# Local attention steps in pairs on four quarters of TensorE, in a fused attention and two-layer feed-forward kernel

## Chip, cores and metric

The program runs on 1 core of one Trainium2 chip. The metric is device time in microseconds of that core, from the start of the program to its end; lower is better. Three runs of the kernel before have a median of 943.49 µs (941.63 to 943.52).

## The reference

```python
def _attn_ref(q, k, v):                      # B, H, S, D = 4, 8, 576, 64
    factor = 4
    scale = 1.0 / np.sqrt(D)
    q_d, k_d, v_d = (mean over 4 neighbouring tokens of q, k, v)
    out_up = np.repeat(sm_attn(q_d, k_d, v_d), factor, axis=2)
    mask = np.abs(pos[:, None] - pos[None, :]) < factor
    scores = np.where(mask, scale * q @ k.T, -1e9)
    out_local = softmax(scores) @ v
    return out_up + out_local
...
x = attn_out.transpose(0, 2, 1, 3).reshape(2304, 512)
g = x @ w_gate
x = (g * sigmoid(g) * (x @ w_val)) @ w_out   # 512 -> 1536 -> 512
h = np.maximum(x @ w_in, 0.0)
out = (h * h) @ w_out2                       # 512 -> 2048 -> 512
```

Per head there is a "global" attention over 144 pooled tokens, and a "local" one in which a query sees only the keys fewer than 4 positions away. Their sum, 2304 tokens of 512, goes through two feed-forward layers. All of it is float32.

## The kernel before

**Precision.** Feed-forward products are made of three single-pass products each (`three`, lines 1045 to 1047): high part by high part, high by low, low by high. Those lines carry most of TensorE's time. The attention matmuls take float32 operands directly; in the trace one such matmul is two records.

**Local attention.** The 576 tokens of a batch are cut into ten blocks of 56 or 58 queries (`EDGES`, `BLOCKS`), each with a window of 64 keys. A block has 8 heads: four pairs `hp`, and in a pair one head on partitions 0–63 and one on 64–127 (`h2`). One step (`local_task`, line 613) does one or two blocks: `nb` is 1 or 2. Per batch there are six steps, of blocks (0,1), (2,3), (4) in the first half and (5), (6,7), (8,9) in the second. The stages of a step, in order:

- `scores` (line 635): for batches 0 and 1 (`MASK_PE` is 2) the mask first enters the bank by a bf16 matmul (L644); then, per block and head pair, two matmuls of 64 rows by 64 columns (L649), the first on rows 0–63 into output partitions 0–63, the second on rows 64–127 into output partitions 64–127. For batches 2 and 3 VectorE adds the mask instead (`masked`, L661).
- the softmax stages on VectorE and ScalarE (lines 550 to 588),
- `trans` (L686): two 128x128 transposes per block on TensorE, and `turned` (L694): eviction to SBUF by ScalarE,
- `pv` (line 696): per block eight matmuls of 64 rows by 64 columns over 58 or 56 queries (L707), again alternating between rows and output partitions 0–63 and 64–127,
- `to_x` (L725): VectorE adds the pooled attention `g` and writes the tile `xt`.

The values come by `values`: one DMA for batch 0 (L674), two per block for the other batches (L681), into one of two `vw` buffers. The load may start once the step's scores have been issued. Transposes wait for `turn`: the global steps of the same half must have come far enough.

The global steps (`global_tasks`, `global_task`) have scores in L797, which alternate between rows 0–63 and 64–127 and write output partitions 0–71 of one bank for the first and of another for the second, and value products in L835, which use rows 0–71 and alternate between output partitions 0–63 and 64–127 of one bank.

**What sets the order.** Nothing is scheduled at run time. A planner inside the program (`Order`, `Task`, `Stage`) simulates the engines with costs written in the code, and emits the instructions in the order that its simulation gives; each engine then executes its own list in order. Every stage has an engine, a cost and the buffers that it takes and gives: four PSUM banks `att`, two `gv`, two `y`; five `p` tiles, two `pt`, two `vw`, two `xt`. Attention has priority on TensorE up to 2 µs at a stretch (`ATT_MAX`), then products go first. A local step's scores are planned at 0.63 µs per block and 0.737 with masks, its value products at 0.64 per block. A DMA is planned at its size over 70e3 elements per µs, plus a flight of 1.7 µs (`FLIGHT`) and 3.5 µs of slack (`SLACK`); the values of two blocks count as 1.87 µs. Between 40 and 100 µs the planner fills long waits for a bank with dummy matmuls (`bank`, L81). The first 40 µs have other dummies (L1251).

**Weights.** Weights arrive as words that ScalarE and VectorE turn into high and low tiles (`bit_stages`, L367 to L384; `pair_task`, L1355 to L1366). While attention runs, some of this work is done ahead, and the tiles are written to DRAM and fetched later: `N_FIRST` groups of eight tiles of the second layer (two calls of `pair_task` each, on two sources each), and `N_PUT` blocks of five tiles of the second half of the first layer (one `pair_task` and one `w_task`; spilled to `f_sp`). The other blocks are converted after attention has ended (`late_`), and the other groups later still.

**Order of the stages over the span.** Batch 0's first half and its global steps stand in the first 45 µs with little else; from then to 270 µs attention is interleaved with the first half of the first layer; then come the second half of the first layer and the second layer, which have no attention.

Of the kernel before, what the change touches and what calls it, by code (L numbers as in the profile page):

```python
# [1 line left out]

# [1 line left out]

# [15 lines left out]
B, H, S, D = 4, 8, 576, 64  # L20
NTOK, DM, FF1, FF2 = B * S, H * D, 1536, 2048
HP = H // 2
# [3 lines left out]
WIN = 64  # L26
# [33 lines left out]
HALF0 = (0, S - HALF)  # L60
# [3 lines left out]
def attn_moe_kernel(ctx: ExitStack, tc: tile.TileContext, qT, kT, vw, vin, vp, qp, kp, qs, ks, vs, maskc, masks, identc, wB, wC, out):  # L64
    nc = tc.nc
# [32 lines left out]
    def dma(size):  # L98
        return size / RATE
# [27 lines left out]
    def after(ts):  # L127

        return max([0.0] + [t.ready for t in ts]) if all(t.done for t in ts) else None
# [392 lines left out]
    def x_of(token):  # L522
        return max(t for t in range(NT1) if X_AT[t] <= token)
# [87 lines left out]

    early_room = []

    def local_task(b, i, ins, due, bls=(0, 1), early=False):

        u = {}
        first, last = early and i == 0, early and i == 2
# [2 lines left out]
        def room(k, size=None):  # L620
# [5 lines left out]
        nb, b0 = len(bls), bls[0]  # L626
# [5 lines left out]
        if len(set(kinds)) == 1:  # L632
            runs = [(0, n, kinds[0])]

        def scores():
            half = int(t00 >= S // 2)
            q, k, o = q_t[b, half], k_t[b, half], HALF0[half]
# [7 lines left out]
            for c, (_, _, q0, w0) in enumerate(blocks):  # L645
                for hp in range(HP):
                    for h2 in range(2):
                        r = slice(64 * h2, 64 * h2 + 64)
                        nc.tensor.matmul(  # L649
                            u["s"][r, c * HP + hp],  # L650
                            q[r, hp, q0 - o : q0 - o + WIN],
                            k[r, hp, w0 - o : w0 - o + WIN],
                            start=not mask_pe,
                            stop=not mask_pe or c * HP + hp == n - 1,
                        )

        def masked():
            u["p"] = p_tile(128, n, WIN)
# [11 lines left out]
        def values():  # L670
            v = room(10, 8 * D) if last else att.tile([128, 8 * D], F32, tag="vw", bufs=N_V, name="vw")
            if b < NB:
                u["v"] = v.rearrange("p (a h l d) -> p l a h d", a=2, h=2, d=D)
                nc.sync.dma_start(out=v, in_=vw[b * NPAIR + i].rearrange("p a h l d -> p (a h l d)"))  # L674
                return
            u["v"] = v.rearrange("p (l h a d) -> p l a h d", h=2, a=2, d=D)
            heads = vs[b - NB].rearrange("p f -> (p f)").rearrange("(r h t d) -> r t h d", r=2, h=4, d=D)
            for r in range(2):
                for bl, (_, _, _, w0) in zip(bls, blocks):
                    o = v[64 * r : 64 * r + 64].rearrange("p (l h d) -> p l h d", l=2, d=D)[:, bl]  # L680
# [15 lines left out]
        def pv():  # L696
            for t in tiles:
                x_tile(t)
            ps = u["ps"] = bank("att")
            pt = u["pt"].rearrange("p (b a h k) -> p b a h k", b=nb, a=2, h=2)  # L700
            for c, (t0, t1, q0, _) in enumerate(blocks):
                for hpp in range(2):
                    for h2 in range(2):
                        for r in range(2):
                            rr = slice(64 * r, 64 * r + 64)
                            o = (2 * h2 + hpp) * 128 + t0 - t00
                            nc.tensor.matmul(  # L707
                                ps[rr, o : o + t1 - t0],
                                u["v"][rr, bls[c], hpp, h2, :],
                                pt[rr, c, hpp, h2, t0 - q0 : t1 - q0],  # L710
                                start=True,
                                stop=True,
                            )

        def to_x():
            at = t00
# [14 lines left out]
                at = end  # L731

        tiles = range(x_of(b * S + t00), x_of(b * S + t11 - 1) + 1)

        def g_need():
            return [t for c in range(t00 * 2 // S, (t11 - 1) * 2 // S + 1) for t in g_tasks[b, c]]

        def ready():
            when, room = after([v_in] + g_need()), x_room(tiles)
            return None if when is None or room is None else max(when, room)  # L740

        def turn():

            return 0.0 if early or all(t.at > len(t.stages) - 4 for t in g_need()) else None

        v_take = () if last else ("v",)
        v_in = Task([Stage("d", dma(128 * 512) * (1 if b < NB else 2), values, v_take, cond=lambda: task.ready)], due)
        if mask_pe:
            cost, share = 0.737 * nb, 0.74
            softmax = softmax_stages(u, n, 128, WIN, "s", float(D) ** -0.5, 1, False, ("att",))  # L750
        else:
            cost, share = 0.63 * nb, 0.68
            softmax = [Stage("v", dve(n * WIN), masked, (), ("att",))]
            softmax += softmax_stages(u, n, 128, WIN, "p", 1.0, 1, False, ())
        p_take, pt_take, pt_give = ("p",), ("pt",), ("pt",)
        if early:
            p_take, pt_take = ("xs",) * 3 * first, ()
            pt_give = tuple(lambda k=k: ("xs", early_room[k][0]) for k in range(3)) if last else ()
        task = Task(
            [Stage("t", cost, scores, ("att",) + p_take, (), lambda: after(ins + [consts]), share)]  # L760
            + softmax
            + [
                Stage("t", 0.22 * nb, trans, ("att",) + pt_take, p_take[-1:] * (not early), turn, 0.98),
                Stage("a", act(n * WIN, True), turned, (), ("att",)),
                Stage(
                    "t", 0.64 * nb, pv, ("att",), pt_give + v_take, ready, 0.62
                ),
                Stage("v", dve(232 * nb), to_x, (), ("att",)),
            ],
            due,  # L770
            then=[v_in],
        )
        for t in tiles:
            x_parts[t].append(task)
        return task

    def global_tasks(b, ins, due, combos, end=False):

# [89 lines left out]
            g_tasks[b, qc].append(task)  # L868
        return task

    att_tasks = {}

    def x_due(token):
        tile = token / T1
# [41 lines left out]
    def queue_att(b):  # L916
# [69 lines left out]
            ]  # L986
            return list(glob_tasks[b, qc])

        halves = ((0, (0, 1)), (1, (0, 1)), (2, (0,))), ((2, (1,)), (3, (0, 1)), (4, (0, 1)))
        ts = globals_(0) + globals_(1) if b >= NB else []  # L990
        for qc in range(2):
            first = globals_(qc) if b < NB else []
            early = EARLY if first and qc == 0 else 0.0
            loc_tasks[b, qc] = [local_task(b, i, ins[qc], due[qc] - early, bls, early > 0) for i, bls in halves[qc]]
            ts += loc_tasks[b, qc] + first if early else first + loc_tasks[b, qc]
        queues["att"] += ts
        att_tasks[b] = ts


    xh_t, x_at, x_tasks, y_t, downs = {}, {}, {}, {}, []  # L1000
# [320 lines left out]
    last_scores = lambda: 0.0 if all(t.at for t in att_tasks[B - 1]) else None  # L1321
# [855 lines left out]
    def rows(t, r0, c):  # L2177
        return t[r0 + 2 * c : r0 + 2 * c + 2].rearrange("r p d -> p r d")
# [265 lines left out]
```

## Time and profile before

| | |
|---|---|
| median of 3 runs | 943.49 µs (941.63 to 943.52) |
| the profiled execution's own time | 944.18 µs |
| its span in the profile | 942.4 µs |
| granted TensorE clock, mean | 0.999 of full speed |
| instructions | 22566 |

How to read it: the span runs from the first to the last instruction of the program in the profile; the execution's own time has 1.8 µs more. Busy time is the time in which an engine has an instruction in flight, and matmuls are pipelined, so records overlap and 100% busy doesn't mean that no more would fit. PE is TensorE's matmuls, PEld its weight loads, DVE VectorE, ACT ScalarE, POOL GpSimd, SP the queue that issues most DMAs. L649 is line 649 of the kernel. In rows by window the five busy times stand in the order PE, PEld, DVE, ACT, POOL.

### The profile page before, as it was taken

What the parts mean: (1) busy time and instruction counts of PE and PEld (TensorE: products, weight loads), DVE (VectorE), ACT (ScalarE), POOL (GpSimd) and SP (SyncE); (2) the same over time, 40 slices, a digit from 0 to 9 for tenths busy, and PEclk for the clock granted to TensorE, in tenths of its full rate; (3) what the DMA queues carried; (4) which work ended last, traced back from release to release, by engine and by line L of the source; (5) the groups of instructions that cost most, each with busy time, mean ns of one, the idle gap of its engine ahead of it and who ended that gap; (6) DMA issues with size and microseconds to landing.
All of it is one profiled execution on the core that took longest, in us unless ns stands there. A gap on an engine that the chain in (4) does not pass through costs nothing.

```text
span 942.4 us, 22566 instructions
## 1 busy us (share of the span) xinstructions
PE 931.2 (99%) x8929; PEld 907.0 (96%) x8929; DVE 757.3 (80%) x1875; ACT 584.5 (62%) x1368; POOL 23.8 (3%) x31
## 2 busy tenths in 40 slices
PE   8999999999999999999999999999999999999997
PEld 6888999999999999999999999999999999999997
DVE  6998969878978878788796999978777666776865
ACT  3878667657667888456542675757565645555553
POOL 0102102000000000000000000000000000000000
PEclk9999999999999999999999999999999999999999
DMA  9998969586678857166553638624315864516131
GB/s 278 262 286 225 243 186 239 179 270 183 225 269 312 265 172 252 50 220 204 187 185 101 211 138 312 244 81 180 126 77 178 316 230 171 180 67 247 47 133 68
DMA packets 101205, 183.82 MB, mean 195 GB/s; under 512 B 22380, under 2 KB 60012, under 8 KB 101100
## 3 DMA queue, kind: packets, MB, share of 16 engines
q1 hardware_dynamic: 97644, 174.42, 54.8%
q0 software_dynamic: 3456, 7.96, 4.8%
q8 instruction: 70, 1.15, 0.5%
q14 instruction: 35, 0.29, 0.1%
HBM read 120.75 MB, written 61.60 MB: 193 GB/s over the span
## 4 chain that ended last, share of the span: by engine, by line
PE 92%; DVE 2%; ACT 2%; DMA 2%; SPq 1%; issue 0%; DVEq 0%
PE gv L1045 11%; PE gv L1047 10%; PE gv L1046 10%; PE y L1045 8%; PE y L1046 8%; PE y L1047 8%; PE att L1983 6%; PE att L1982 6%; PE att L1981 6%; PE att L1046 3%; PE att L1047 3%; PE att L1045 3%; PE att L707 2%; PE att L797 2%; PE att L649 1%; PE y L1251 1%
## 5 line engine op out<-in xcount | busy, mean ns | idle before, releaser
L1045 PE MATMUL gv<-xs,wg 128*128 128x256 f32 x880 | 250.4, 285 | 0.1
L1046 PE MATMUL gv<-xs,wg 128*128 128x256 f32 x880 | 246.9, 281 | 0.0
L1047 PE MATMUL gv<-xs,wg 128*128 128x256 f32 x880 | 246.9, 281 | 0.0
L1045 PEld LDWEIGHTS gv<-xs,wg 128*128 128x128 f32 x880 | 166.2, 189 | 2.1 <-issue 0.4
L1046 PEld LDWEIGHTS gv<-xs,wg 128*128 128x128 f32 x880 | 166.1, 189 | 0.0
L1047 PEld LDWEIGHTS gv<-xs,wg 128*128 128x128 f32 x880 | 166.0, 189 | 0.0
L2132 ACT ACTIVATE f<-rr 128x256 fp32r<-128x256 f32 (+2 forms) x200 | 88.1, 467 | 62.9 <-PE att L1983 25.7
L1983 PE MATMUL att<-wg,f 128*128 128x256 f32 x432 | 122.5, 284 | 0.5 <-DVE f L2135 0.4
L1982 PE MATMUL att<-wg,f 128*128 128x256 f32 x432 | 122.0, 282 | 0.0
L1981 PE MATMUL att<-wg,f 128*128 128x256 f32 x432 | 121.7, 282 | 0.3 <-ACT f L2132 0.3
L2135 DVE TENSOR_TENSOR f<-rr,f 128x512 fp32r<-128x512 f32 (+2 forms) x200 | 94.0, 488 | 27.2 <-ACT f L2132 26.5
L2056 ACT ACTIVATE rr<-rr 128x512 f32<-128x512 f32 (+1 forms) x144 | 80.2, 557 | 31.4 <-DVE rr L2059 29.2
L1045 PE MATMUL y<-xs,wg 128*128 128x256 f32 x336 | 94.6, 281 | 1.1 <-ACT ys L1228 1.1
L1046 PE MATMUL y<-xs,wg 128*128 128x256 f32 x336 | 94.5, 281 | 0.0
L1047 PE MATMUL y<-xs,wg 128*128 128x256 f32 x336 | 94.4, 281 | 0.0
L1981 PEld LDWEIGHTS att<-wg,f 128*128 128x128 f32 x432 | 81.8, 189 | 0.7 <-ACT f L2132 0.7
L1983 PEld LDWEIGHTS att<-wg,f 128*128 128x128 f32 x432 | 81.2, 188 | 1.4 <-DVE f L2135 1.3
L1982 PEld LDWEIGHTS att<-wg,f 128*128 128x128 f32 x432 | 81.5, 189 | 0.0
L2141 DVE TENSOR_TENSOR rr<-rr 128x256 f32<-128x256 f32 (+1 forms) x160 | 62.3, 393 | 7.0 <-ACT rr L2056 4.7
L1045 PEld LDWEIGHTS y<-xs,wg 128*128 128x128 f32 x336 | 63.6, 189 | 1.4 <-ACT ys L1228 1.3
L1047 PEld LDWEIGHTS y<-xs,wg 128*128 128x128 f32 x336 | 63.5, 189 | 0.0
L1046 PEld LDWEIGHTS y<-xs,wg 128*128 128x128 f32 x336 | 63.5, 189 | 0.1
(149 smaller groups left out, 2317.2 us busy)
## 6 DMA issues: line engine op xcount, KB each, us to landing
wst<-wB SPq DMA_DIRECT2D x36, 512.0 KB, 4.9
w_sp<-tmp SPq DMA_DIRECT2D x36, 512.0 KB, 3.8
wg<-w_sp SPq DMA_DIRECT2D x36, 512.0 KB, 5.1
wst<-wC SPq DMA_DIRECT2D x32, 512.0 KB, 5.0
y_sp<-ys SPq DMA_DIRECT2D x29, 512.0 KB, 4.5
xf_sp<-xs SPq DMA_DIRECT2D x24, 512.0 KB, 2.7
xs<-xf_sp SPq DMA_DIRECT2D x24, 512.0 KB, 5.4
ys<-y_sp SPq DMA_DIRECT2D x20, 512.0 KB, 6.7
```

The lines of the kernel that those rows point to most:

```text
L707: nc.tensor.matmul(ps[rr, o : o + t1 - t0], u["v"][rr, bls[c], hpp, h2, :], pt[rr, c, hpp, h2, t0 - q0 : t1 - q0], start=True, stop=True,)
L797: nc.tensor.matmul(us[h2]["s"][:, ci], q, kd_t[b][r, hp, :], start=start, stop=stop)
L1045: nc.tensor.matmul(o, w[:, 0], x[:, 0], start=start, stop=False, skip_group_check=more)
L1046: nc.tensor.matmul(o, w[:, 0], x[:, 1], start=False, stop=False, skip_group_check=more)
L1047: nc.tensor.matmul(o, w[:, 1], x[:, 0], start=False, stop=stop, skip_group_check=more)
L1981: nc.tensor.matmul(o, h, w[:, 0], start=first and not again and c == 0, stop=False, skip_group_check=again)
L1982: nc.tensor.matmul(o, h, w[:, 1], start=False, stop=False, skip_group_check=again)
L1983: nc.tensor.matmul(o, l, w[:, 0], start=False, stop=end, skip_group_check=again)
L2056: return lambda: nc.scalar.activation(out=whole(f, c0), in_=whole(f, c0), func=func)
L2132: nc.scalar.activation(out=fac(k, 0), in_=source(), func=AF.Copy)
L2135: nc.vector.tensor_tensor(out=fac(k, 1), in0=source(), in1=fac(k, 0).bitcast(F32), op=ALU.subtract)
L2141: go = lambda: nc.vector.tensor_tensor(out=o(), in0=a(), in1=b(), op=op)
```

## The change

Two local steps become two lanes of one pair. In batches 1 to 3 the pairs are blocks (0,1) with (2,3), (4) with (5), and (6,7) with (8,9); in batch 0 only the last two steps are paired, and the other steps go through the same code with one lane. A pair has one scores stage: the matmuls of the lanes alternate, and lane 1 writes its output into the other half of the partitions (`h2 ^ lane`) and into a bank of its own, so that rows 0–63 feed output partitions 0–63 for lane 0 and 64–127 for lane 1, and rows 64–127 the other way round. Head pairs of lane 1 are swapped as well (`hp ^ lane`), and its values are loaded with the halves of the partitions exchanged, so that after the value products, exchanged once more, each head stands where it stood. Softmax, transposes and `to_x` stay one per lane. The value products of both lanes are one stage again, which takes two banks and waits for both lanes' values, for all global steps that either lane needs and for room in the `xt` tiles. Transposes of a pair also wait until the value products of the pair before have been issued (`val_before`). In batch 0 lane 1's values are two DMAs instead of one. The planner's costs are 0.63 per block of a lane for the scores of one or two lanes, plus 0.107 per block and lane with masks, and 0.64 for the values.

The constants of the weights change from `N_FIRST, N_DIRECT, N_PUT = 4, 2, 1` to `3, 2, 2`.

```diff
-N_FIRST, N_DIRECT, N_PUT = 4, 2, 1
+N_FIRST, N_DIRECT, N_PUT = 3, 2, 2
...
+        def score(at):
...
+            for h2 in range(2):
+                nc.tensor.matmul(
+                    u["s"][rows(h2 ^ lane), c * HP + (hp ^ lane)],
+                    q[rows(h2), hp, q0 - o : q0 - o + WIN],
+                    k[rows(h2), hp, w0 - o : w0 - o + WIN],
...
+                if lane:
+                    for r in range(2):
+                        nc.sync.dma_start(out=v[rows(r)], in_=whole[rows(1 - r)])
+                else:
+                    nc.sync.dma_start(out=v, in_=whole)
...
-                    nc.sync.dma_start(out=o, in_=heads[r, w0 : w0 + WIN])
+                    nc.sync.dma_start(out=o, in_=heads[r ^ lane, w0 : w0 + WIN])
...
+        def value(at):
...
+            for r in range(2):
+                o = (2 * h2 + hpp) * 128 + t0 - t00
+                nc.tensor.matmul(
+                    u["ps"][rows(r ^ lane), o : o + t1 - t0],
+                    u["v"][rows(r), bls[c], hpp, h2, :],
+                    pt[rows(r), c, hpp, h2 ^ lane, t0 - q0 : t1 - q0],
...
+    def local_task(b, parts, ins, due, early=False):
+        lanes = [local_lane(b, i, bls, lane, early) for lane, (i, bls) in enumerate(parts)]
...
+        def scores():
+            for x in lanes:
+                x.masks()
+            for at in range(n):
+                for x in lanes:
+                    x.score(at)
+
+        def pv():
+            for x in lanes:
+                x.begin()
+            for at in range(4 * nb):
+                for x in lanes:
+                    x.value(at)
+
+        def ready():
+            when, room = after(v_in + mids + g_need), x_room(tiles)
+            return None if when is None or room is None else max(when, room)
+
+        def turn():
+
+            if before and not early and not before.done:
+                return None
+            return 0.0 if early or all(t.at > len(t.stages) - 4 for t in g_need) else None
+
+        cost = 0.63 * nb + nl * 0.107 * nb * (b < MASK_PE)
...
+        v_in = [Task([Stage("d", x.load, x.values, v_take, cond=lambda: head.ready)], due) for x in lanes]
+        head = Task([Stage("t", cost, scores, ("att",) * nl + p_take, (), lambda: after(ins + [consts]), 0.7)], due)
...
+        val = Task([Stage("t", 0.64 * nb, pv, ("att",) * nl, pt_give + v_take * nl, ready, 0.7)], due)
+        ends = [Task([Stage("v", dve(232 * nb), to_x, (), ("att",), lambda: after([val]))], due) for x in lanes]
...
-        halves = ((0, (0, 1)), (1, (0, 1)), (2, (0,))), ((2, (1,)), (3, (0, 1)), (4, (0, 1)))
+        both = (0, 1)
+        ends_ = [(3, both), (4, both)]
+        if b < NB:
+            lanes = [[(0, both)], [(1, both)], [(2, (0,))]], [[(2, (1,))], ends_]
+        else:
+            lanes = [[(0, both), (1, both)]], [[(2, (0,)), (2, (1,))], ends_]
```

## Rows read from the trace of the kernel before

**Rows 1.** The page, part 1: busy µs, share of the span, instructions.

```profile
PE 931.2 (99%) x8929; PEld 907.0 (96%) x8929; DVE 757.3 (80%) x1875; ACT 584.5 (62%) x1368; POOL 23.8 (3%) x31
```

**Rows 2.** Windows, all engines: stretch, length, busy (instructions); then clock, DMA share, GB/s.

```profile
40.00:75.00 35.00, 34.98 (x455) 31.28 (x456) 33.12 (x94) 27.31 (x82) 3.43 (x4) 1.00 0.95 299
75.00:270.00 195.00, 194.50 (x2438) 182.39 (x2437) 163.96 (x430) 130.31 (x345) 15.63 (x18) 1.00 0.76 217
270.00:345.00 75.00, 75.00 (x642) 75.00 (x641) 62.26 (x135) 62.66 (x126) 0.00 (x0) 1.00 0.80 274
```

**Rows 3.** Waits of PE: waiter <- releaser, µs, times, longest.

```profile
PE att L707 <- DMA vw<-vs: 0.2, 1, 0.2
```

**Rows 4.** Lines, PE: busy µs, mean ns, then idle before.

```profile
L649 PE MATMUL att<-kT,qT 64*64 64x64 f32 x640 | 23.2, 221 | 1.3 <-DMA qT<-qT 1.3
...
L707 PE MATMUL att<-pt,vw 64*64 64x58 f32 (+1 forms) x560 | 20.4, 221 | 0.2 <-DMA vw<-vs 0.2
...
L81 PEld LDWEIGHTS <-zeros 128*128 128x128 bf16 x28 | 2.6, 97 | 0.5 <-issue 0.2
```

**Rows 5.** Timeline, PE, 96.2–97.9, 104.0–106.4, 267.8–269.4 µs: start, length, line, tiles, records.

```profile
96.39 0.28 PE L1047 MATMUL y<-hh,wg 128*128 128x256 f32 x1
96.60 1.14 PE L707 MATMUL att<-pt,vw 64*64 64x58 f32 x32
...
105.80 0.39 PE L1045 MATMUL gv<-xs,wg 128*128 128x256 f32 x1
106.02 0.28 PE L1046 MATMUL gv<-xs,wg 128*128 128x256 f32 x1
106.14 0.28 PE L1047 MATMUL gv<-xs,wg 128*128 128x256 f32 x1
...
267.99 1.14 PE L707 MATMUL att<-pt,vw 64*64 64x58 f32 x32
```

**Rows 6.** Chain that ended last, in order of time: start, length, what.

```profile
46.68 0.61 PE att L649 x16
...
47.61 1.08 PE att L649 x32
...
143.41 2.01 PE att L649 x64
```

**Rows 7.** Timeline, PE, from 50.970 to 51.079; then to 51.090 and 51.137 alike.

```profile
50.97 0.27 PE L649 MATMUL att<-kT,qT 64*64 64x64 f32 x2
...
50.97 0.33 PE L649 MATMUL att<-kT,qT 64*64 64x64 f32 x4
```

**Rows 8.** Timeline, PE, 73.740 to 73.859 and 73.870; 125.180 to 125.366 and 125.380 µs.

```profile
73.75 0.28 PE L835 MATMUL att<-pt,vd 72*64 72x72 f32 x2
...
73.75 0.35 PE L835 MATMUL att<-pt,vd 72*64 72x72 f32 x4
...
125.19 0.35 PE L797 MATMUL att<-kd,qd 64*72 64x144 f32 x2
...
125.19 0.47 PE L797 MATMUL att<-kd,qd 64*72 64x144 f32 x4
```

**Rows 9.** Lines by form, DVE, weight conversion: busy µs, mean ns.

```profile
L379 DVE SCALAR_TENSOR_TENSOR wf<-wst,bits 128x512 int32<-128x512 int32 x68 | 46.5, 685 | 3.2 <-ACT wst L376 2.7
...
L1366 DVE TENSOR_TENSOR wf<-wf 128x256 f32<-128x256 f32 x88 | 36.8, 418 | 0.8
...
L1359 DVE TENSOR_TENSOR tmp<-wf,tmp 128x512 fp32r<-128x512 f32 x39 | 26.7, 684 | 4.6 <-ACT tmp L1355 4.1
```

**Rows 10.** DMA issues: queue, count, KB each, median µs to landing.

```profile
f_sp<-tmp SPq DMA_DIRECT2D x4, 512.0 KB, 5.0
```

**Rows 11.** Line L681: issues, ns min/median/max; and µs to landing.

```profile
L681 SPq DMA_DIRECT2D vw<-vs x60: 596/616/1705, 79.7 to 261.6; - x60
...
DMA to landing us min/median/max: 2.3/3.0/7.2
```

**Rows 12.** Waits of SP's queue: waiter <- releaser, µs, times, longest.

```profile
SPq L681 <- PE att L707: 14.2, 5, 6.9
```

More of the change, by code (lines that the diff above doesn't have):

```diff
@@ L1 @@
 from contextlib import ExitStack
+from types import SimpleNamespace
 import numpy as np
@@ L625, in room, with rows @@
             return flat[:, k : k + (size or n * WIN)]
-        nb, b0 = len(bls), bls[0]
+        def rows(r):
+            return slice(64 * r, 64 * r + 64)
+        nb = len(bls)
         n = nb * HP
@@ L633, in local_task, with masks @@
             runs = [(0, n, kinds[0])]
-        def scores():
-            half = int(t00 >= S // 2)
-            q, k, o = q_t[b, half], k_t[b, half], HALF0[half]
+        def masks():
             u["ps"] = bank("att")
@@ L644, in scores @@
                 nc.tensor.matmul(u["s"][:, c0:c1], ident_b, m, start=c0 == 0, stop=False)
[L645 to L655, printed above, removed]
+        def score(at):
+            half = int(t00 >= S // 2)
+            q, k, o = q_t[b, half], k_t[b, half], HALF0[half]
+            c, hp = at // HP, at % HP
+            _, _, q0, w0 = blocks[c]
+            for h2 in range(2):
[3 more added lines that the diff above has]
+                    k[rows(h2), hp, w0 - o : w0 - o + WIN],
+                    start=not mask_pe,
+                    stop=not mask_pe or at == n - 1,
+                )
         def masked():
@@ L673, in values @@
                 u["v"] = v.rearrange("p (a h l d) -> p l a h d", a=2, h=2, d=D)
-                nc.sync.dma_start(out=v, in_=vw[b * NPAIR + i].rearrange("p a h l d -> p (a h l d)"))
+                whole = vw[b * NPAIR + i].rearrange("p a h l d -> p (a h l d)")
+                if lane:
[3 more added lines that the diff above has]
+                    nc.sync.dma_start(out=v, in_=whole)
                 return
@@ L733, in local_task @@
         tiles = range(x_of(b * S + t00), x_of(b * S + t11 - 1) + 1)
-        def g_need():
-            return [t for c in range(t00 * 2 // S, (t11 - 1) * 2 // S + 1) for t in g_tasks[b, c]]
+        g_need = [t for c in range(t00 * 2 // S, (t11 - 1) * 2 // S + 1) for t in g_tasks[b, c]]
+        if mask_pe:
+            softmax = softmax_stages(u, n, 128, WIN, "s", float(D) ** -0.5, 1, False, ("att",))
+        else:
+            softmax = [Stage("v", dve(n * WIN), masked, (), ("att",))]
+            softmax += softmax_stages(u, n, 128, WIN, "p", 1.0, 1, False, ())
@@ new lines, in local_lane @@
+        load = dma(128 * 512) * (1 if b < NB else len(bls))
+        return SimpleNamespace(**locals())
+    def local_task(b, parts, ins, due, early=False):
+        lanes = [local_lane(b, i, bls, lane, early) for lane, (i, bls) in enumerate(parts)]
+        nb, n, nl = lanes[0].nb, lanes[0].n, len(lanes)
+        tiles = range(lanes[0].tiles[0], lanes[-1].tiles[-1] + 1)
+        g_need = list(dict.fromkeys(t for x in lanes for t in x.g_need))
+        before = val_before[0]
+        def scores():
[10 more added lines that the diff above has]
+                    x.value(at)
@@ L748, in local_task @@
[L748 to L755, printed above, removed]
-        if early:
-            p_take, pt_take = ("xs",) * 3 * first, ()
-            pt_give = tuple(lambda k=k: ("xs", early_room[k][0]) for k in range(3)) if last else ()
@@ L759, in local_task @@
[L759 to L772, printed above, removed]
@@ L773, in local_task @@
-        for t in tiles:
-            x_parts[t].append(task)
-        return task
+            if before and not early and not before.done:
+                return None
+            return 0.0 if early or all(t.at > len(t.stages) - 4 for t in g_need) else None
+        cost = 0.63 * nb + nl * 0.107 * nb * (b < MASK_PE)
+        p_take, pt_take, pt_give, v_take = ("p",) * nl, ("pt",), ("pt",) * nl, ("v",)
+        if early:
+            p_take, pt_take = ("xs",) * 3 * lanes[0].first, ()
+            pt_give = ()
+            if lanes[0].last:
+                pt_give = tuple(lambda k=k: ("xs", early_room[k][0]) for k in range(3))
+                v_take = ()
@@ new lines, in local_task @@
+        v_in = [Task([Stage("d", x.load, x.values, v_take, cond=lambda: head.ready)], due) for x in lanes]
+        head = Task([Stage("t", cost, scores, ("att",) * nl + p_take, (), lambda: after(ins + [consts]), 0.7)], due)
+        mids = []
+        for x in lanes:
+            x.softmax[0].cond = lambda: after([head])
+            mids.append(
+                Task(
+                    x.softmax
+                    + [
+                        Stage("t", 0.22 * nb, x.trans, ("att",) + pt_take, () if early else ("p",), turn, 0.98),
+                        Stage("a", act(n * WIN, True), x.turned, (), ("att",)),
+                    ],
+                    due,
+                )
+            )
@@ L777, in global_tasks @@
+        val = Task([Stage("t", 0.64 * nb, pv, ("att",) * nl, pt_give + v_take * nl, ready, 0.7)], due)
+        ends = [Task([Stage("v", dve(232 * nb), x.to_x, (), ("att",), lambda: after([val]))], due) for x in lanes]
+        head.then = [*v_in, *mids, val, *ends]
+        if not early:
+            val_before[0] = val
+        for x, end in zip(lanes, ends):
+            for t in x.tiles:
+                x_parts[t].append(end)
+            att_ends[b].append(end)
+        return head
     def global_tasks(b, ins, due, combos, end=False):
@@ L869, in global_task @@
         return task
-    att_tasks = {}
+    att_tasks, att_heads, att_ends = {}, {}, {b: [] for b in range(B)}
     def x_due(token):
@@ L993, in queue_att @@
             early = EARLY if first and qc == 0 else 0.0
-            loc_tasks[b, qc] = [local_task(b, i, ins[qc], due[qc] - early, bls, early > 0) for i, bls in halves[qc]]
+            loc_tasks[b, qc] = [local_task(b, x, ins[qc], due[qc] - early, early > 0) for x in lanes[qc]]
             ts += loc_tasks[b, qc] + first if early else first + loc_tasks[b, qc]
+        if b >= NB:
+            loc_tasks[b, 0].append(loc_tasks[b, 1][0])
         queues["att"] += ts
-        att_tasks[b] = ts
+        att_heads[b] = ts
+        att_tasks[b] = ts + att_ends[b]
     xh_t, x_at, x_tasks, y_t, downs = {}, {}, {}, {}, []
@@ L1320, in attn_moe_kernel @@
     turned_all = lambda: after(sum(att_tasks.values(), sum(x_parts, [])))
-    last_scores = lambda: 0.0 if all(t.at for t in att_tasks[B - 1]) else None
+    last_scores = lambda: 0.0 if all(t.at for t in att_heads[B - 1]) else None
     late_ = Task([apart("tmp", 5, last_scores), apart("bits", 1), Stage(None, 0.0, late, (), (), turned_all)])
```

32 lines of the change are left out of this document (11 added, 21 removed).

## The prediction

> **What bounds the kernel now.** I read the engines' shares first: TensorE 99% of the span, VectorE 80%, ScalarE 62% [rows 1]. Then busy time by stretch, since a share over the whole span hides stages. In 75–270 µs, where batches 1 to 3 pass through attention beside the first feed-forward layer, TensorE is busy 194.50 of 195 µs at full granted clock; VectorE stands at 163.96, the 16 DMA engines at 0.76. In 40–75 µs VectorE is at 33.12 of 35 and DMA at 0.95: there three resources are nearly full together. In 270–345 µs TensorE still has 75.00 of 75 [rows 2]. Third, the waits of TensorE: the value products (L707) waited for their `vw` loads 0.2 µs, once, in the whole run [rows 3]. So from 75 µs on TensorE's own instructions set the pace, and what is taken from them should leave the end of the program, while the 75 µs of 270–345, products alone and without a gap, show that it isn't short of work [rows 2].
>
> How much stands in the two lines that change: the score matmuls (L649) make 640 records and 23.2 µs of busy time, the value products (L707) 20.4 µs for batches 0 (second half) to 3 [rows 4]. The first three steps of batch 0 stay single in the change.
>
> **What a burst costs.** These matmuls come in bursts. A burst of 32 records starts 0.21 µs after the last product where products follow each other at 0.12, and the second product behind a burst comes 0.22 after the first instead of 0.12 [rows 5]. Inside, 16 records take 0.61, 32 take 1.08, 64 take 2.01 µs [rows 6]: (2.01 − 0.61)/48 = 29.2 ns per record and 0.14 fixed. With 0.09 before and 0.10 behind, a separate burst has 0.33 µs of fixed cost.
>
> Why 29.2 ns? Two records start within 11 ns of each other (two in flight at 51.079 µs, four at 51.090), and then no other until after 51.137; the modelled end moves by 0.06 µs [rows 7]. So a round is about 58 ns with one record on each of the two quarters in use; each quarter needs 58 ns per record, and issuing takes 7 to 11 of it. The sequencer has room for two more records in each round.
>
> Would two more quarters run beside them? Two halves of that are in the trace. L835 puts both records on the same rows and on different column halves: two in flight, then four within 11 ns, 0.07 later. L797 puts them on different rows and on the same output partitions of two banks: again pairs [rows 8]. The change needs both at once, which no row shows. Bounds for a round of four: 58 ns (free) and 117 (they take turns, as now). I take 58, the end nearest to both rows.
>
> The Trainium skill, page "TensorE: Matmul & The Clock Gate", Part 3, section "The mechanism", says that a weight load overlaps matmuls in flight only when the row group differs; with quarters in the order 0/0, 1/1, 0/1, 1/0 of rows and columns that would make the second pair queue behind the first and save the fixed costs alone. The column-half pairs of L835 in [rows 8] disagree with it. The same page, Part 1, section "Wait — 56ns, not 53.3ns?", gives a floor of about 25 ns from start to start; by it a round of four would be 100 ns and the sum over the records 272 × 17 = 4.6 instead of 15.9 µs. The pairs within 11 ns in [rows 7] disagree with that as well.
>
> **The sum.** Pairs: one in batch 0 (16 rounds), three in each of batches 1 to 3 (16 + 8 + 16). So 136 rounds of two vanish for scores and 136 for values, and as many rounds of four stay: 272 × 58.4 ns = 15.9 µs. Bursts: I count 16 score and 17 value bursts between 47.5 and 269 µs, the first at 47.61 in [rows 6], the last at 267.99 in [rows 5]; ten of each remain, 13 × 0.33 = 4.3, less where two stand beside each other already; I take 4. Mask matmuls, transposes, softmax, the eviction by ScalarE and the additions into `xt` keep their count and size: 0. Together 20 µs off TensorE.
>
> What doesn't reach the end: batch 0's pair falls into 47–70 µs, where the planner put 28 dummy matmuls (L81) because nothing was ready [rows 4]; its share, 16 of 136 rounds twice plus its bursts, 2.5 µs, only makes more of those. Net 17.5.
>
> The redivided weights (one group of eight tiles fewer in `N_FIRST`, one block of five tiles more in `N_PUT`) move conversion work. A group costs VectorE 4 × 0.685 + 8 × 0.418 + 6 × 0.684 + 2 × 0.418 = 11.0 µs, a block 2 × 0.685 + 4 × 0.418 + 3 × 0.684 + 0.418 for its pair and 0.685 + 0.684 for the third weight, 6.9 [rows 9]. So VectorE has 4.1 µs less before attention ends. In 75–270 its load goes from 164/195 to 160/178 = 90%, which stays under TensorE. In exchange 2.25 MB more goes out and comes back, five issues each way at 5.0 µs to landing [rows 10], in a stretch with DMA at 0.80 [rows 2]: hidden by the products of 270–345, and without that cover late by the 5.0 µs of one landing. I take 0.
>
> Added waits: a value burst now needs both lanes' `vw` buffers, which are all there are, so the next pair's loads (eight issues of 0.6 µs on the sync queue, 3.0 median and 7.2 at most to land [rows 11]) can start only behind it. Batch 0's pair has one issue more than now, 0.6 at that row's price, on a queue that TensorE doesn't wait for there. The next pair's transposes also wait for it (`turn`). Behind a waiting value burst stand the products of TensorE, behind a waiting load the weight and q/k loads of the queue, which is held 14.2 µs in 5 such waits already [rows 12]. Bounds: 0 if the products that the planner puts between cover it, 3 µs per pair if not (4.9 + 7.2 against the 9 µs that the planner's own load cost gives two lanes), 27 in all. The 0.2 µs of [rows 3] is the nearest row: 0.5.
>
> Sum: 944.18 (the profiled execution: span 942.4 and 1.8 around it) − 17.5 + 0.5 = 927.2; the median of the runs is 0.7 lower, so **926.5 µs**.
>
> **Rivals.** *Partial rate or partial cover:* a round of four takes 87 to 100 ns, or VectorE's 90% turns into TensorE waits in 75–120 µs. With 87 the record sum is 272 × 30 = 8.2, 7.7 less: 934; with 100 it is 11.3 less: 938. For: VectorE is at 33.12 of 35 just before. Against: TensorE was busy 99.7% of 75–270 beside it [rows 2], and nothing in [rows 7] shows such a step. The 25-ns floor of the Trainium skill's page above would give the 938. *Quarters take turns:* 117 ns per round; only 4 µs of fixed cost goes, 1.5 of it under dummies and waits: 941. This is the case in which the change doesn't do what it says; against it stand the pairs of [rows 8], for it that no row has all four. The rule on row groups of the Trainium skill's page above would give this case. *Slower, by the value loads:* TensorE stands at each of nine paired value bursts for `vw`, 3 µs each: 926.5 + 27 = 953. It decides from 17/9 = 1.9 µs per pair upwards. For: two buffers, both taken; [rows 12]. Against: [rows 3], and the 75 µs of products in hand at 270 µs [rows 2].
>
> **Numbers.** Full rate with small waits 0.60 (922–931); partial 0.20 (931–939); turns 0.10 (939–943); slower 0.10 (943–955). The range 919 to 940 leaves out the last two and reaches 7 below the forecast for fixed costs of 4.3 fully won, batch 0's share won too, and 4 µs of better cover. 0.2% of this kernel, 1.9 µs, is about what a measurement can tell from no change; turns falls half inside it. Faster 0.84, same 0.06, slower 0.10.
>
> **What would show it.** Right: the score and value lines have fewer, denser bursts; 64 records of a pair in about 1.08 µs (14.6 ns each), four starts within some 25 ns and then a gap to 58; TensorE still full from 75 to 330 µs; the last value burst near 250 µs instead of 267.99. Wrong: 64 records in 2.0 µs (turns), 1.5 (partial); waits of the value matmuls on `vw` over 5 µs in sum; L81 dummies well over 28; VectorE at its limit with TensorE idle between 75 and 200 µs; or idle TensorE around 330–360 µs on late weights.

## The result, and the profile after

The changed kernel takes 931.43 µs (median of 4 runs, 931.01 to 931.92) against 943.5 before: a ratio of 0.9876, 95% interval 0.9859 to 0.9893, 12.1 µs faster. The forecast was 926.5 within 919 to 940. Direction and range held. Up to the end of attention the sum held too; behind it the kernel loses some 3 µs again, in stages for which the sum had taken 0.

In the changed kernel the scores are L657, the value products L720, the mask matmuls L649, the dummies L82, the products L1099 to L1101 and, in the second layer, L2035 to L2037. The page, part 1, answers to [rows 1]:

```profile
PE 914.3 (98%) x8950; PEld 892.1 (96%) x8950; DVE 756.1 (81%) x1875; ACT 584.6 (63%) x1368; POOL 23.7 (3%) x31
```

The same windows as in [rows 2], and two later ones:

```profile
40.00:75.00 35.00, 34.34 (x463) 30.57 (x462) 32.78 (x92) 28.00 (x82) 2.17 (x3) 1.00 0.96 287
75.00:270.00 195.00, 193.25 (x2569) 183.34 (x2569) 167.23 (x439) 132.35 (x350) 15.58 (x18) 1.00 0.77 218
270.00:345.00 75.00, 73.87 (x627) 73.46 (x627) 60.81 (x131) 60.83 (x122) 0.00 (x0) 1.00 0.76 256
345.00:400.00 55.00, 53.56 (x451) 53.16 (x450) 46.04 (x109) 32.52 (x71) 0.00 (x0) 1.00 0.56 202
500.00:600.00 100.00, 98.23 (x822) 97.32 (x821) 92.72 (x217) 66.09 (x142) 0.00 (x0) 1.00 0.69 237
```

The later two in the kernel before:

```profile
345.00:400.00 55.00, 53.87 (x455) 53.46 (x454) 44.62 (x107) 36.70 (x77) 0.00 (x0) 1.00 0.45 149
500.00:600.00 100.00, 99.58 (x837) 98.83 (x836) 86.87 (x208) 57.53 (x125) 0.00 (x0) 1.00 0.54 191
```

TensorE is still nearly full everywhere. New gaps are 1.75 µs in 75–270, 1.3 at 363 µs and 1.4 more in 500–600; the 1.1 in 270–345 is a wait that the kernel before has in 345–400. Lines of PE, as in [rows 4]:

```profile
L657 PE MATMUL att<-kT,qT 64*64 64x64 f32 x640 | 14.1, 222 | 0.9 <-DMA qT<-qT 0.9
...
L720 PE MATMUL att<-pt,vw 64*64 64x58 f32 (+1 forms) x560 | 11.0, 221 | 1.8 <-issue 1.8
...
L82 PE MATMUL gv<-zeros 128*128 128x256 bf16 x39 | 4.6, 273 | 0.0
...
L82 PE MATMUL att<-zeros 128*128 128x256 bf16 x10 | 1.3, 274 | 0.0
```

As many records as before, 640 and 560, stand in 14.1 µs instead of 23.2 and in 11.0 instead of 20.4; 49 dummies instead of 28. The chain of work (start, length, what), as in [rows 6]:

```profile
84.73 1.09 PE att L657 x64
89.89 0.62 PE att L657 x32
...
96.69 1.09 PE att L657 x64
97.78 0.92 PE att L720 x63
98.71 1.75 issue
...
254.73 1.09 PE att L720 x64
```

64 records now take the 1.09 µs that 32 took, and 32 take 0.62 where 16 took 0.61 [rows 6]: rounds of four at the length of rounds of two. The last value burst starts at 254.73 µs; the forecast had it near 250. The timeline from 130.70 to 130.80 µs shows one round, four starts together (compare [rows 7]):

```profile
130.75 0.28 PE L720 MATMUL att<-pt,vw 64*64 64x58 f32 x4
```

The chain shows something else: one value burst that follows a score burst directly stops for 1.75 µs before its last record, for nothing that the profile names. The waits of PE, and those of the sync queue for `vw` (compare [rows 3] and [rows 12]):

```profile
PE att L720 <- issue: 1.8, 1, 1.8
PE att L1099 <- ACT h L1859: 1.3, 1, 1.3
PE att L2035 <- ACT wg L1409: 1.2, 1, 1.2
```

```profile
SPq L694 <- PE att L720: 30.0, 5, 18.5
```

In this row the queue stands twice as long as before; in the kernel before, 8.2 µs more of that line's waits are put down to the transposes (L686), which the changed kernel doesn't have. No matmul of TensorE waited for `vw`.

### The profile page after: what moved, and what is told of

The parts are those of the page before. It is cut to its first block, busy times and chain, and to the rows that moved or that the text cites. A ratio compares the mean times of both kernels' runs of the same rounds, so it can differ in the third digit from the quotient of the medians.

```text
span 929.2 us, 22649 instructions
## 1 busy us (share of the span) xinstructions
PE 914.3 (98%) x8950; PEld 892.1 (96%) x8950; DVE 756.1 (81%) x1875; ACT 584.6 (63%) x1368; POOL 23.7 (3%) x31
## 4 chain that ended last, share of the span: by engine, by line
PE 94%; DVE 3%; ACT 1%; issue 1%; DMA 1%; SPq 0%; DVEq 0%
PE gv L1099 11%; PE gv L1101 11%; PE gv L1100 11%; PE y L1099 9%; PE y L1100 8%; PE y L1101 8%; PE att L2037 6%; PE att L2036 6%; PE att L2035 6%; PE att L1100 3%; PE att L1101 3%; PE att L1099 3%; PE att L843 2%; PE att L657 1%; PE att L720 1%; PE att L881 1%
## 5 line engine op out<-in xcount | busy, mean ns | idle before, releaser
L1099 PE MATMUL gv<-xs,wg 128*128 128x256 f32 x880 | 250.6, 285 | 0.0
L1101 PE MATMUL gv<-xs,wg 128*128 128x256 f32 x880 | 247.2, 281 | 0.1
L1099 PEld LDWEIGHTS gv<-xs,wg 128*128 128x128 f32 x880 | 166.4, 189 | 1.9 <-issue 0.6
L1101 PEld LDWEIGHTS gv<-xs,wg 128*128 128x128 f32 x880 | 166.2, 189 | 0.3 <-DVE wg L427 0.3
L2186 ACT ACTIVATE f<-rr 128x512 fp32r<-128x512 f32 (+2 forms) x200 | 88.2, 467 | 62.1 <-PE att L2037 24.2
L2035 PE MATMUL att<-wg,f 128*128 128x256 f32 x432 | 121.8, 282 | 1.5 <-ACT wg L1409 1.2
L2037 PE MATMUL att<-wg,f 128*128 128x256 f32 x432 | 122.6, 284 | 0.1
L1099 PE MATMUL y<-xs,wg 128*128 128x256 f32 x336 | 94.5, 281 | 1.1 <-ACT ys L1282 1.1
L1101 PE MATMUL y<-xs,wg 128*128 128x256 f32 x336 | 94.5, 281 | 0.0
L2035 PEld LDWEIGHTS att<-wg,f 128*128 128x128 f32 x432 | 81.9, 190 | 1.9 <-ACT wg L1409 1.4
L2037 PEld LDWEIGHTS att<-wg,f 128*128 128x128 f32 x432 | 81.2, 188 | 1.0 <-DVE f L2189 0.8
L1099 PEld LDWEIGHTS y<-xs,wg 128*128 128x128 f32 x336 | 63.6, 189 | 1.3 <-ACT ys L1282 1.3
L1101 PEld LDWEIGHTS y<-xs,wg 128*128 128x128 f32 x336 | 63.6, 189 | 0.0
```

The costliest lines, as they stand in the source:

```text
L1099: nc.tensor.matmul(o, w[:, 0], x[:, 0], start=start, stop=False, skip_group_check=more)
L1101: nc.tensor.matmul(o, w[:, 1], x[:, 0], start=False, stop=stop, skip_group_check=more)
L2035: nc.tensor.matmul(o, h, w[:, 0], start=first and not again and c == 0, stop=False, skip_group_check=again)
L2037: nc.tensor.matmul(o, l, w[:, 0], start=False, stop=end, skip_group_check=again)
L2186: nc.scalar.activation(out=fac(k, 0), in_=source(), func=AF.Copy)
```

## The experiments

Each kernel below is the changed kernel with the edit shown, or the kernel before where that is said; all ratios are to the kernel before on the same chip.

### Two quarters for both lanes

```diff
-        lanes = [local_lane(b, i, bls, lane, early) for lane, (i, bls) in enumerate(parts)]
+        lanes = [local_lane(b, i, bls, 0, early) for lane, (i, bls) in enumerate(parts)]
```

> The changed kernel with one edit: both lanes of a pair use lane 0's two quarters, and nothing is exchanged; the planner's costs, the order of the work and the division of the weights stay as changed. If the gain is the second pair of quarters: the 64 records of a pair take about 2.0 us instead of 1.09, the 272 rounds of 58 ns come back on TensorE, and all but batch 0's share (which then takes the place of dummies) shows: 14 us more, 945 us, with a range of 942 to 948, not faster than the kernel before. If the gain came from pairing alone (fewer separate bursts, another order): 931 to 934.

946.14 µs, ratio 1.0024 (1.0015 to 1.0034): 14.7 slower than the changed kernel. Its chain:

```profile
86.62 2.01 PE att L657 x64
...
99.96 2.01 PE att L657 x64
101.97 1.86 PE att L720 x64
```

So with this division of the weights nothing is left of the gain without the second pair of quarters: pairing by itself ends 2.6 µs slower than before, though it has fewer bursts. The rival that put the gain on pairing is out. One limit: the planner still counts 1.26 µs for these 64 records, which here take 2.01, so the order is one made for four quarters; a plan made for two wasn't tested.

### Lane after lane

```diff
-            for at in range(n):
-                for x in lanes:
+            for x in lanes:
+                for at in range(n):
                     x.score(at)
...
-            for at in range(4 * nb):
-                for x in lanes:
+            for x in lanes:
+                for at in range(4 * nb):
                     x.value(at)
```

> The changed kernel with one edit: in the two loops over a pair's matmuls all of lane 0 is issued before lane 1, so that the two lanes still use four quarters but don't alternate in the program. If TensorE takes its matmuls nearly in order, with room for a few waiting ones: 64 records take 2.0 us, and the time goes to 945 (942 to 948). If it could look 32 records ahead, 64 records would stay at 1.1 and the time at 931 to 932.

941.47 µs, ratio 0.998 (0.997 to 0.9989). Its chain:

```profile
85.73 1.84 PE att L657 x62
91.66 0.91 PE att L657 x30
```

A burst takes 1.84 µs: 0.17 under two quarters' 2.01, three rounds of 58 ns. So about six records of lane 1 run beside the last ones of lane 0; the expected 2.0 and 945 missed this overlap at the seams. Quarters alone don't do it: the program must alternate between them.

### The old division of the weights

```diff
-N_FIRST, N_DIRECT, N_PUT = 3, 2, 2
+N_FIRST, N_DIRECT, N_PUT = 4, 2, 1
```

> The changed kernel with the constants of the weights as before (four groups first, one block put). If the two waits of the products in the later layers (1.3 us at 363 us on the eviction, 1.7 us at 573 us on directly converted tiles) come from the new division, they vanish and VectorE has 4 us more to do in 75 to 270 us: 928 to 930, unless TensorE waits there. If the new division is what keeps VectorE out of TensorE's way, waits of 2 us and more appear between 75 and 270 us: 933 to 936. If the division does nothing, as the prediction had it: 931 to 932.

939.62 µs, ratio 0.9953 (0.9941 to 0.9966): 8.2 slower than the changed kernel, more than any of the three theories. Its waits of PE and its window:

```profile
PE att L1099 <- ACT h L1859: 6.3, 3, 2.8
```

```profile
345.00:400.00 55.00, 46.95 (x363) 45.01 (x362) 45.76 (x107) 38.24 (x80) 0.00 (x0) 0.97 0.49 156
```

TensorE is idle 8.05 of 55 µs where the changed kernel has 1.44, and the granted clock dips; the 1.2 µs wait on `wg` in the second layer is gone, as expected. What is late is `h`, the gated result of the first layer, not a weight.

### The new division alone, in the kernel before

```diff
-N_FIRST, N_DIRECT, N_PUT = 4, 2, 1
+N_FIRST, N_DIRECT, N_PUT = 3, 2, 2
```

> The kernel before with one edit: the new division of the weights (three groups first, two blocks put). The prediction took 0 for it: within 1.5 us of 943.5. If the later waits of the changed kernel come from it: 945 to 947, with the same waits of the products near 370 and 580 us.

965.03 µs, ratio 1.0229 (1.0212 to 1.0245). The constants that save 8 µs with pairs cost 21.5 without. Its window in the second layer:

```profile
500.00:600.00 100.00, 91.33 (x710) 88.89 (x709) 81.15 (x191) 55.05 (x116) 0.00 (x0) 0.93 0.68 237
```

127 product records fewer than before's 837 fit into this stretch: 8.7 µs idle and a granted clock of 0.93.

### The other two divisions

`N_FIRST, N_PUT` at 4, 2 and at 3, 1.

> The changed kernel with one constant as before (four groups first) and the other as changed (two blocks put). If the blocks put alone decide the waits at 345 to 385 us and the groups first alone those near 573 us: neither has more than 1.3 us in sum, and the time is 931.4 - 1.7 = 929.7 us. If VectorE, which then converts 11 us more before attention ends, holds TensorE up there: waits of 2 us and more between 75 and 345 us, 933 us and more.

> The changed kernel with the other constant as before (three groups first, one block put). If the two constants act each on its own stage: waits of 6 to 8 us at 345 to 385 us as with the old division, and 1.7 us near 573 us: 939.6 + 1.7 = 941.3 us. If the sum of VectorE's work before attention's end is what counts, the second half of the first layer gets more of VectorE and its waits shrink: 933 to 936.

947.69 µs (ratio 1.0053, 1.0041 to 1.0065) and 948.35 (1.0057, 1.0044 to 1.007). Both are 16 to 17 slower than the changed kernel. The first has most of its waits in the first layer, the second in the second; the two windows, the first fence with 4, 2:

```profile
345.00:400.00 55.00, 47.01 (x343) 44.89 (x344) 43.41 (x100) 38.25 (x76) 0.00 (x0) 0.92 0.59 196
```

```profile
500.00:600.00 100.00, 86.91 (x646) 83.27 (x645) 78.03 (x181) 55.26 (x116) 0.00 (x0) 0.91 0.63 216
```

The constants don't act each on its own stage, and no rule "more ahead is better", or worse, orders the four: of four divisions one fits this plan.

### Both edits: two quarters and the old division

> The changed kernel with both edits: two quarters for both lanes, and the old division of the weights. It completes the square of quarters and division. If the old division hurts the changed kernel only because TensorE, with four quarters, comes to the second half of the first layer before its weights do: with two quarters the waits at 345 to 385 us fall from 7.8 to under 2 us, and the time is 943 to 945, under the 946.1 of two quarters with the new division. If the pairs' order of the work as such makes the old division late: those waits stay at 6 us and more, and the time is 952 to 955.

952.58 µs, ratio 1.0096 (1.0079 to 1.0113). The theory that faster attention comes before its weights falls. The waits of PE:

```profile
PE att L1099 <- ACT h L1859: 6.3, 3, 2.8
```

the same 6.3 µs, three times, as with four quarters, though TensorE comes there some 14 µs later. The longest of them in the timeline, here and then in the kernel with four quarters and the old division:

```profile
383.68 0.39 PE L1099 MATMUL att<-h,wg 128*128 128x256 f32 x1 [2.77 <-ACT h L1859]
```

```profile
370.07 0.39 PE L1099 MATMUL att<-h,wg 128*128 128x256 f32 x1 [2.77 <-ACT h L1859]
```

2.77 µs in both. The planner's costs are the same in the two kernels, and so is the order that it writes: in the two traces all 1875 instructions of VectorE and all 1368 of ScalarE follow each other alike. ScalarE ahead of it in the second kernel:

```profile
367.34 0.77 ACT L373 ACTIVATE bits<-wst 128x512 fp8e5<-128x512 uint8 x1
...
368.22 0.41 ACT L1859 ACTIVATE h<-ss 128x256 fp32r<-128x256 f32 x1
368.53 0.67 ACT L377 ACTIVATE wst<-wst 128x512 f32<-128x512 f32 x1
369.08 0.63 ACT L1409 ACTIVATE wg<-wf 128x512 fp32r<-128x512 f32 x1
369.60 0.41 ACT L1859 ACTIVATE h<-ss 128x256 fp32r<-128x256 f32 x1
```

Two weight-conversion steps (L377, L1409) stand between two evictions of `h`, and TensorE waits for the second; they take about 1 of the 2.77 µs, and another conversion (L373) stands ahead of the first. Which conversion stands between which evictions is written by the planner. So the wait goes with the written order, not with the time at which TensorE arrives. The square of the four kernels:

| | old division | new division |
|---|---|---|
| kernel before, no pairs | 943.5 | 965.0 |
| pairs on two quarters | 952.6 | 946.1 |
| pairs on four quarters | 939.6 | 931.4 |

### The stall of 1.75 µs

The first dummies are split, so that all later instructions of TensorE move back in its program: 64 places in one kernel, 128 in the other.

```diff
+        left = [32]
 
         def go():
+            if left[0]:
+                left[0] -= 1
+                for c in range(2):
+                    nc.tensor.matmul(ps[:, c * 128 : c * 128 + 128], zeros[:, :128], zeros[:, :128], start=True, stop=True)
+                return
```

> The changed kernel with the first dummies of 256 columns split into two of 128 (26 to 32 of them), so that all later instructions of TensorE stand 52 to 64 places further in its program; nothing else. If the stall of 1.8 us at 98.7 us is TensorE running out of fetched instructions: it leaves the last record of that value burst, to some 26 to 32 records earlier, or vanishes; the time is 929.6 to 931.4 us. If it belongs to that record (its bank, its buffer): 63 records, then 1.8 us, then one, as now; 931.4.

930.94 µs, ratio 0.9875 (0.9862 to 0.9887). All 32 were split: 8982 matmul records instead of 8950. The chain there:

```profile
96.59 1.09 PE att L657 x64
97.68 0.46 PE att L720 x31
98.14 1.54 issue
99.68 0.69 PE att L720 x33
```

The stall has left the 63rd record for the 31st: 32 records, 64 instructions earlier, exactly as far as the program moved. So it belongs to a place in the program, not to that record's operands. In the changed kernel's trace one packet of an instruction queue falls into the microsecond in which the stall begins (DMA view, 98 to 99 µs):

```profile
q8 instruction: 1, 0.02, 5.5%
```

With 64 places that packet starts in 97 to 98 µs, earlier like the stall.

With 64 for 32 in the same lines:

> The changed kernel with the first 64 dummies split into two of 128 columns each, so that later instructions of TensorE stand 128 places further; nothing else. With 64 places the stall moved from the 63rd to the 31st record of the value burst at 98 us, 32 records or 64 instructions earlier, and kept 1.54 us. If a fixed place in the program starves and only a stretch of more than 64 dense records runs into it: the place is now the seam between the score and the value burst, the stall vanishes, 929.4 us. If any place within the two bursts starves alike: 1.5 us again, at the seam, and 930.9.

929.4 µs, ratio 0.9858 (0.9844 to 0.9872). The chain:

```profile
96.60 1.09 PE att L657 x64
97.69 0.94 PE att L720 x64
```

No stall, and the time that was expected. No packet of that queue starts between 92 and 101 µs here. TensorE waiting for its own instructions, where two dense bursts stand back to back, fits all three kernels; bursts of 64 alone never show it in them. The three other divisions on four quarters have the two bursts and the stall as well, after 62 or 63 records (1.1 to 1.6 µs); on two quarters, where the same 128 records take 3.87 µs, there is none. How far ahead instructions are fetched wasn't measured. This version, the changed kernel with 64 split dummies, is the fastest of the study, 2.0 µs under the changed one.

### A third `vw` buffer

`N_V` from 2 to 3.

> The changed kernel with three vw buffers instead of two. The sync queue stood 30 us for these buffers, but no TensorE matmul waited for vw: the queue's hold falls by a third or more, and the time stays within 1 us of 931.4. If the late weight tiles at 363 and 573 us were held up by that queue: those waits shrink by 1 us or more and the time goes to 929 to 930.

944.34 µs, ratio 1.0011 (1.0003 to 1.002): 12.9 slower, which neither theory allowed. The queue's wait for `vw` did fall from 30.0 µs:

```profile
SPq L694 <- PE att L720: 10.7, 4, 4.0
```

but the planner, with a buffer more, wrote another order. TensorE is idle 3.5 µs in 40–75 and 8.25 in 500–600:

```profile
40.00:75.00 35.00, 31.48 (x416) 26.94 (x413) 32.09 (x90) 27.05 (x83) 2.52 (x3) 0.95 1.00 294
...
500.00:600.00 100.00, 91.75 (x734) 89.66 (x734) 86.87 (x204) 61.66 (x131) 0.00 (x0) 0.97 0.69 237
```

So it doesn't tell what the buffer itself is worth.

### Batch 0 unpaired

```diff
-            lanes = [[(0, both)], [(1, both)], [(2, (0,))]], [[(2, (1,))], ends_]
+            lanes = [[(0, both)], [(1, both)], [(2, (0,))]], [[(2, (1,))], [(3, both)], [(4, both)]]
```

> The changed kernel with batch 0's last two steps unpaired again. By the prediction's term batch 0's pair won nothing, since dummies took its place: two bursts more of each kind, 2.5 us, and some 20 dummies fewer than 49; the time stays within 0.7 us of 931.4. If the pair was worth its 2.5 us: 934. If the changed order makes weight tiles of the later layers late, as the other divisions did: 936 and more, with waits of the products on converted tiles.

938.98 µs (933.72 to 943.98 over 11 runs), ratio 0.9951 (0.9934 to 0.9968). No single wait decides. By the table in the next section 2.6 of the 7.6 µs are lost before attention ends, and 5.0 behind it. There this kernel has 1.8 µs in three waits at 343 to 348 µs, 1.5 on `h` at 368, and, behind waits at 368 and 580, two stretches of 5 µs at a clock of 0.66 (370–375) and 0.69 (582–587) that start 28 and 31 records where 44 are usual; the changed kernel has the waits at 363 and 573 alone. The runs differ in such dips: the fastest, 933.72 µs, had a mean clock of 0.999, the slowest 0.992. There are 47 dummies, not the 29 expected, since 19 others came in later; the 2.6 µs speak against a pair in batch 0 that wins nothing, but its worth stays open.

## Why the prediction was right, and where it was wrong

**Where the time was won and lost.** All these kernels have the same 6576 product records, and in all of them attention is over before the 1500th starts. So the start of that product, counted in the traces, tells what was won by then, and the start of the last one what is left. Both are given less those of the kernel before (304.25 and 937.57 µs), in µs, from one profiled execution each:

| kernel | product 1500 | last product | lost between |
|---|---|---|---|
| changed kernel | −16.1 | −13.1 | 3.1 |
| two quarters | −2.5 | +2.1 | 4.6 |
| old division | −15.5 | −4.4 | 11.1 |
| two quarters, old division | −1.9 | +8.9 | 10.8 |
| kernel before, new division | −2.0 | +19.8 | 21.8 |
| `N_FIRST, N_PUT` 4, 2 | −16.7 | +2.6 | 19.3 |
| `N_FIRST, N_PUT` 3, 1 | −17.0 | +4.2 | 21.3 |
| lane after lane | −6.4 | −1.9 | 4.5 |
| 64 dummies split | −18.1 | −15.1 | 3.1 |
| third `vw` buffer | −13.6 | −0.2 | 13.3 |
| batch 0 unpaired | −13.5 | −5.5 | 8.0 |

The chains of three kernels show the same lead at product 1957, which in each follows a wait of 1.1 µs on `ys`; the kernel before, the changed one, and two quarters:

```profile
359.15 0.39 PE y L1045
```

```profile
343.02 0.39 PE y L1099
```

```profile
356.61 0.39 PE y L1099
```

**Four quarters at full rate: right, and without them there is no gain.** The step "Bounds for a round of four: 58 ns (free) and 117 … I take 58" held: 1.09 µs for 64 records. By product 1500 the second pair of quarters is worth 13.6 µs with either division (−16.1 against −2.5, −15.5 against −1.9), against 15.9 in the sum; 1.75 and 1.64 of the difference are the stall, which the sum didn't have. At the end the worth is 14.7 µs (946.1 to 931.4) or, with the old division, 13.0 (952.6 to 939.6). The rule on row groups of the Trainium skill's page "TensorE: Matmul & The Clock Gate", Part 3, section "The mechanism", would have given two quarters' 2.01 µs; this trace disagrees. So it does with the floor of 25 ns per start in Part 1: four start within one step of 58.

**Fewer bursts, 4 µs less 1.5 under dummies and waits: right.** Pairs on two quarters save this alone, 2.5 µs by the forecast's rival of quarters that take turns (941). By product 1500 they are 2.5 and 1.9 µs ahead of the kernel before. That they end 2.6 and 9.1 µs slower than it comes from the later stages.

**"The redivided weights: I take 0", and nothing for the stages without attention: the step that failed.** Up to product 1500 the division moves little (1.5 µs at most with pairs on four quarters, 2.0 without pairs). Behind it, it decides: with pairs on four quarters the four divisions lose 3.1, 11.1, 19.3 and 21.3 µs. The number of quarters hardly counts there (3.1 and 4.6 with the new division, 11.1 and 10.8 with the old). One such window, on two quarters with the old division:

```profile
345.00:400.00 55.00, 46.94 (x362) 44.74 (x362) 46.32 (x106) 42.57 (x86) 0.00 (x0) 0.97 0.57 182
```

6.9 µs less busy than before's 53.87, at a clock of 0.97; 93 records fewer. The sum priced the mask matmuls, transposes and softmax by count and size, and the conversions by VectorE's time before attention ends (4.1 µs less). Those prices can't show it: a new grouping of tasks or another division makes the planner write a new order for what follows, and 100 µs after the last attention step a product meets an eviction behind a conversion. In the changed kernel the new waits are 1.3 µs on `h` at 363 and 1.7 on weight tiles at 573.

**The sum.** Forecast: −15.9 − 4 + 2.5 + 0.5, −17. By product 1500: −16.1, or −17.9 without the stall. The loss behind it, taken as 0, is 3.1, so −13.1 is left between these two executions and −12.1 between the medians. So the mechanism was right and the total near for the reason given; that the new division loses 3.1 µs, and not 11 to 21 like the other three, is luck as far as the prediction goes, which had no reason to choose among them. The terms don't add, either: in the square above, pairing on two quarters costs 9.1 µs with the old division and gains 18.9 with the new.

**Added waits on `vw`, 0.5: the lower bound held.** TensorE waited for `vw` not at all; the slower rival (3 µs at each pair) is out, though the queue's hold in that row doubled to 30.0 µs. That held queue cost TensorE no wait.

**Dummies:** 49 instead of 28; 4.6 + 1.3 µs busy for 49 makes 2.5 for the 21 more, an estimate, as forecast; the forecast had also listed them as a sign of being wrong. But they aren't the price of quarters that come too early: with two quarters the same 49 are there. They, too, are written by the plan.

**VectorE at 90%:** TensorE's only idle time in 75–270 is the stall, 195 − 193.25 = 1.75 µs, so the cover held. The forecast's mark for "wrong", idle TensorE around 330–360 µs on late weights, was near the right place for another cause (363 µs, on `h`), and the late weights came at 573 µs.

## What to carry over

Small float32 matmuls on separate 64x64 quarters overlap fully when they alternate in the program; that part can be forecast from the start-to-start times of two quarters. In a kernel whose order is planned offline, the plan itself is a term: small edits to constants, buffers or grouping moved this one by 6 to 21 µs, mostly in stages that they don't touch, so a change should be forecast with that spread, timed with its neighbours (constants, buffers), and taken apart with one edit at a time. When a gain is near the forecast, check the terms one by one before believing the reasons, and compare kernels at the same amount of finished work, not only at the end: here that told what the change did from what the new order cost.

## What the runs showed that was not expected

**A dense stretch can starve of instructions.** 1.75 µs after 127 records in 2.0 µs, moved by a shift of the program and gone with a larger one. That the instructions were late is argued from this and from the packets of the instruction queue, not measured by itself.

**A short wait can cost nearly as much again after it.** With two quarters the products wait 1.7 µs in 585–590 and are then granted less clock:

```profile
585.00:590.00 5.00, 3.29 (x26) 2.88 (x25) 4.87 (x12) 2.40 (x6) 0.00 (x0) 1.00 1.03 408
590.00:595.00 5.00, 5.00 (x32) 5.00 (x31) 1.27 (x3) 1.54 (x4) 0.00 (x0) 0.66 0.44 160
```

TensorE is busy throughout the second 5 µs at 0.66, between the 2.4 GHz of 1.00 and the 1.2 GHz of 0.50, and starts 32 records where 44 or 45 are usual: 12 × 0.12 = 1.4 µs more. The changed kernel has the same wait at 573 µs (1.2 and 0.5 µs) and a clock of 1.00 over the whole of 500–600. Why one dips and the other doesn't stays open. In the kernel with four groups first and two blocks put, TensorE is idle for 4.4 of 5 µs, and the next 5 µs are all at 0.50:

```profile
340.00:345.00 5.00, 0.64 (x6) 0.44 (x4) 4.39 (x10) 4.14 (x9) 0.00 (x0) 0.87 0.99 328
345.00:350.00 5.00, 4.43 (x19) 4.14 (x20) 3.95 (x8) 4.00 (x8) 0.00 (x0) 0.50 0.83 242
```
